# Squares of a fused attention kernel from GpSimd to ScalarE, and the gain vectors' load and product moved

## The chip, the cores and the metric

The kernel runs on one core of one Trainium2 chip. A core has five engines that run their own instruction streams: TensorE (PE, matmuls; PEld is its weight load), VectorE (DVE), ScalarE (ACT), GpSimd (POOL) and SyncE (SP, which here only issues DMAs). Each engine works through its own stream in order; semaphores make one wait for another. DMAs are issued from the queues of SP, ACT and POOL. The metric is the device time of one execution in microseconds (us).

## The reference

```python
def rmsnorm(x, g):
    rms = np.sqrt(np.mean(x * x, axis=-1, keepdims=True) + 1e-06)
    return x / rms * g
# q, k, v: (8, 12, 448, 64); g_q, g_k: (64,)
q_n, k_n = (rmsnorm(q, g_q), rmsnorm(k, g_k))
scores = 1.0 / np.sqrt(64) * np.matmul(q_n, k_n.transpose(0, 1, 3, 2))
attn = np.exp(scores - np.max(scores, axis=-1, keepdims=True))
attn = attn / (np.sum(attn, axis=-1, keepdims=True) + 1e-09)
x = np.matmul(attn, v)          # then reshaped to (3584, 768)
a, b = x @ w1, x @ w2           # (768, 1024) each
h = a * b @ w3                  # (1024, 1024)
return (h @ w_out).astype(np.float32)   # (1024, 768)
```

## The kernel before

The work is cut into 24 groups (`NQ`): 8 batches times 3 sets of 4 heads. The 448 tokens of a head lie on 112 partitions with 4 tokens each (`J`). For a group i the kernel

- loads q and k in float32 (`load_qk`, on SP's queue; three buffers each) and v in bfloat16 (`load_v`, on POOL's queue, four buffers);
- prepares q and k two heads at a time (`pr` 0 and 1): the squares of q and of k (`prep_sq`, tile sq), their sums over 64 elements (`prep_red`, DVE, tile ssq, L166), one over the root by a logarithm and an exponential (`prep_alpha`, ACT, tiles lnv and alpha), three multiplies on DVE (`prep_scale`: qtmp L188, qks L195 with the gains g_b, qks L201), and a transpose to qkT, by PE for the first 5 groups (`prep_pe_transpose`, L220) and by a DMA on SP's queue for the others;
- multiplies q and k (`qk_exp`, PE, tile sc, L235, two PSUM buffers of two banks each) and takes the exponential on ACT (tile P, L244);
- multiplies with ones and with v (`pv_set`, PE, tile pv, L259), and scales the result on DVE into xT (L275) with r, the reciprocal of the row sum, from ACT.

Once a batch has its three groups, its feed-forward part is cut into small pieces ("fillers"): pa = x w1 (L315, copied to a_sb by ACT, L323), pb = x w2 (L332, multiplied with a_sb into abT by DVE, L339), and po = abT times w34 (L354, copied by DVE, L361, and stored through SP's queue). w34 = w3 w_out is made once near the start: w3 is transposed by PE in blocks (`w3_transpose`, L293) and multiplied with w_out (`w34_unit`, L301). The weights w_out, w3, w1 and w2 are loaded through POOL's queue; a copy to the tile gate (L408), which needs the last heads of group 0's k, stands in front of them on POOL.

The order is written out by hand. The program goes through slots, four to a group. A slot holds two score blocks with their exponentials, one set of pv products of the group before, up to two pieces of w34 or of the feed-forward part, and then those parts of the preparation of later groups that the tables PREP and SHIFT put there; for groups 7 and up the squares of pr 0 stand at the end of the last slot of group n - 3, those of pr 1 at the end of the first slot of group n - 2. As each engine runs in order, this also sets the order on ACT, DVE and POOL. `N_SQ_ACT` is the number of groups whose squares go to ACT; those of all other groups go to POOL (L159).

Of the kernel before, what the change touches and what calls it, by code (L numbers as in the profile page):

```python
# [10 lines left out]
MULT = mybir.AluOpType.mult  # L11
# [7 lines left out]
def kernel(  # L19
# [13 lines left out]
    nc = tc.nc  # L33

    B, H, S, D = q.shape
    NP = 112
# [22 lines left out]
    big_pool = ctx.enter_context(tc.tile_pool(name="big", bufs=2))  # L59

    N_PE_T = 5
    N_SQ_ACT = 5
    W34_EV = "DA"
    LAG = 4
    SHIFT = [0, 0, 0, -1, -2, -3, -4]
# [16 lines left out]
    gq_b = const.tile([NP, D], FP, name="gq_b")  # L82
    gk_b = const.tile([NP, D], FP, name="gk_b")
    g_b = const.tile([NP, D], BF, name="g_b")
# [13 lines left out]
    def load_qk(i, split=1, k_eng=None):  # L98
        b, m = divmod(i, NQB)
        s = st[i]  # L100
        s["q"] = load_pool.tile([NP, HQ, J, D], FP, tag="q", name="q_sb")
        s["k"] = load_pool.tile([NP, HQ, J, D], FP, tag="k", name="k_sb")
        n = HQ // split
        for h0 in range(0, HQ, n):
            for t_sb, src, eng in (
                (s["q"], q, nc.sync),
                (s["k"], k, k_eng or nc.sync),
            ):
                eng.dma_start(
                    out=t_sb[:, h0 : h0 + n].rearrange("p h j d -> p h (j d)"),  # L110
                    in_=src[b, HQ * m + h0 : HQ * m + h0 + n].rearrange(
                        "h (p j) d -> p h (j d)", j=J
                    ),
                )
# [24 lines left out]
    def load_wout(nh, c):  # L139
        nc.gpsimd.dma_start(  # L140
            out=w_outs[:, 4 * c : 4 * c + 4, nh * NH : (nh + 1) * NH],
            in_=moe_w_out.rearrange("(c p) n -> p c n", p=128)[
                :, 4 * c : 4 * c + 4, nh * NH : (nh + 1) * NH
            ],
        )
# [24 lines left out]
    def prep_alpha(i, h0=0, h1=HQ):  # L170
        s = st[i]
        if h0 == 0:
            s["lnv"] = prep_pool.tile([NP, 2, HQ, J], FP, tag="lnv", name="lnv")
            s["alpha"] = prep_pool.tile([NP, 2, HQ, J], FP, tag="alpha", name="alpha")
        lnv = s["lnv"][:, :, h0:h1]
        nc.scalar.activation(out=lnv, in_=s["ssq"][:, :, h0:h1], func=AF.Ln, bias=eps_t)
        nc.scalar.activation(  # L177
            out=s["alpha"][:, :, h0:h1], in_=lnv, func=AF.Exp, scale=-0.5
        )

    def prep_scale(i, pr, pe=False):
        s = st[i]
        hs = slice(2 * pr, 2 * pr + 2)
        if pr == 0:
            s["qkT"] = qkT_pool.tile([128, 2, 2 * J, NP], BF, tag="qkT", name="qkT")
        alpha = s["alpha"]
        qtmp = prep_pool.tile([NP, J, 2, D], BF, tag="qtmp", name="qtmp")
        nc.vector.tensor_tensor(  # L188
            out=qtmp.transpose([0, 2, 1, 3]),
            in0=s["q"][:, hs],  # L190
            in1=alpha[:, 0, hs].unsqueeze(3).broadcast_to([NP, 2, J, D]),
            op=MULT,
        )
        qks = prep_pool.tile([NP, 2, J, 2, D], BF, tag="qks", name="qks")
        nc.vector.tensor_tensor(  # L195
            out=qks[:, 0],
            in0=qtmp,
            in1=g_b.unsqueeze(1).unsqueeze(1).broadcast_to([NP, J, 2, D]),
            op=MULT,
        )  # L200
        nc.vector.tensor_tensor(  # L201
            out=qks[:, 1].transpose([0, 2, 1, 3]),
            in0=s["k"][:, hs],
            in1=alpha[:, 1, hs].unsqueeze(3).broadcast_to([NP, 2, J, D]),
            op=MULT,
        )
        if pe:
            s["qks", pr] = qks
        else:
            nc.sync.dma_start_transpose(  # L210
                out=s["qkT"][:, pr], in_=qks.rearrange("p t j h d -> p (t j h d)")
            )
# [183 lines left out]

    with tc.manual_schedule():

        nc.vector.memset(warm_t, 0.0)
        nc.vector.memset(eps_t, 64e-6)  # L400
        nc.vector.memset(ones, 1.0)
        load_qk(0, split=2, k_eng=nc.scalar)
        nc.scalar.dma_start(out=gq_b, in_=g_q.unsqueeze(0).broadcast_to([NP, D]))
        nc.scalar.dma_start(out=gk_b, in_=g_k.unsqueeze(0).broadcast_to([NP, D]))
        nc.scalar.preload_act_table_set("natural_log_exp_and_others")
        load_qk(1)
        make_identity(nc, ident)
        nc.gpsimd.tensor_copy(out=gate, in_=st[0]["k"][:, HQ - 1, 0, 0:1])  # L408
        load_wout(0, 0)
        load_wout(0, 1)  # L410
        for c in range(4):
            load_w3(c)
        load_v(0)
        load_wout(1, 0)
        load_wout(1, 1)
        warm(16)
        nc.vector.tensor_tensor(out=gq_b, in0=gq_b, in1=gk_b, op=MULT)
        nc.vector.tensor_scalar(
            out=g_b, in0=gq_b, scalar1=8.0, scalar2=None, op0=MULT
        )  # L420
        for pr in range(2):
            prep_sq(0, pr, on_act=True)
            prep_red(0, pr)
            prep_alpha(0, 2 * pr, 2 * pr + 2)
            prep_scale(0, pr, pe=True)
            if pr == 0:
                prep_pe_transpose(0, 0)

        wq = [lambda c=c: load_w3(c) for c in range(4, CF)]
        wq.insert(2, lambda: load_v(1))  # L430
        wq.append(lambda: load_v(2))
        for h in range(HQ):
            for half in range(2):
                for w, src in ((w1s, moe_w1), (w2s, moe_w2)):
                    wq.append(
                        lambda w=w, src=src, h=h, half=half: load_w12(w, src, h, half)
                    )
        wq.append(lambda: load_v(3))

        w34q = [lambda: w3_transpose(0), lambda: w3_transpose(1)]  # L440
        for fc in range(CF + LAG):
            if fc < CF:
                w34q.append(lambda fc=fc: w34_unit(fc, 0))
            if fc + 2 < CF:
                w34q.append(lambda fc=fc: w3_transpose(fc + 2))
            if fc >= LAG:
                w34q.append(lambda fc=fc: w34_unit(fc - LAG, 1))

        def prep_part(n, part):
            pe = n < N_PE_T  # L450
            if part[:2] == "sq":
                prep_sq(n, int(part[2]), on_act=n < N_SQ_ACT)
            elif part[:3] == "red":
                prep_red(n, int(part[3]))
            elif part == "alpha":
                prep_alpha(n)
            elif part[:2] == "sc":
                prep_scale(n, int(part[2]), pe=pe)
            elif pe:
                prep_pe_transpose(n, int(part[1]))  # L460


        agenda = {}
        for n in range(1, NQ):
            shift = SHIFT[min(n, len(SHIFT)) - 1]
            table = PREP_1 if n == 1 else PREP
            for part, rel in table.items():
                agenda.setdefault(max(0, 4 * n + rel + shift), []).append((n, part))

        for i in range(NQ + 1):  # L470
            for sl in range(4):
                t = 4 * i + sl
                mine = agenda.pop(t, [])
                for n, part in mine:
                    if part == "load":
                        load_qk(n)
                if i < NQ:
                    qk_exp(i, sl)
                if t == 0:
                    prep_pe_transpose(0, 1)  # L480
                seen = len(fillers)
                if i > 0 and sl < 3:
                    pv_set(i - 1, sl)
                fresh = fillers[seen:]
                if sl == 0 and 4 <= i + 1 < NQ:
                    load_v(i + 1)
                for _ in range(4):
                    if wq:
                        wq.pop(0)()
                if t in W34_SLOTS:  # L490
                    for _ in range(W34_SLOTS[t]):
                        if w34q:
                            w34q.pop(0)()
                elif not w34q:
                    left = (14 - t) % 12 + 1
                    old = len(fillers) - sum(1 for f in fillers if f in fresh)
                    fill(min(2, -(-old // left)))
                for n, part in mine:
                    if part[0] == "t":
                        prep_part(n, part)  # L500
                for n, part in mine:
                    if part[0] != "t" and part != "load":
                        prep_part(n, part)
        fill(len(fillers))
# [28 lines left out]
```

## Time and profile before

| | us |
|---|---|
| median of 3 runs | 411.85 (410.21 to 412.54) |
| profiled execution | 408.66 |
| its span, first to last instruction | 406.6 |
| PE busy | 381.0 (94%) |
| DVE busy | 286.8 (71%) |
| ACT busy | 249.8 (61%) |
| POOL busy | 116.7 (29%) |

The mean granted TensorE clock is 0.977 of full speed. A row of the timeline gives start, duration, engine, line, operation, output and inputs, shapes, count, and in brackets how long the engine stood idle before and what released it. A row of the groups gives busy time and mean time of one in ns, then idle time of the engine ahead of it. A row of the waits gives who waited for whom: total us, times, the longest. A row of the chain of waits gives start, duration and what was waited for. A row of the DMA issues gives the median us from issue to landing.

### The profile page before, as it was taken

The page shows a single profiled execution, that of the slowest core. Times are in us where ns is not written, and L with a number is a line of the kernel's source. Part 1 is how long each engine was busy: PE and PEld are TensorE (multiplying, and loading weights), DVE is VectorE, ACT ScalarE, POOL GpSimd, SP SyncE. Part 2 cuts the span into 40 slices and gives each one's busy share as a digit, 9 for nine tenths or more (in the row PEclk, how much of TensorE's full clock was granted, in tenths as well). Part 3 has the DMA queues.
Part 4 walks back from the last instruction along what each step waited for, and adds up shares of the span by engine and source line. Part 5 has one row for each costly group of instructions (what it writes and reads, how often), then busy time and mean ns, then how long its engine had stood idle before and what let it go on. Part 6 is the DMA issues. An engine that isn't in the chain of part 4 may idle for free.

```text
span 406.6 us, 7530 instructions
## 1 busy us (share of the span) xinstructions
PE 381.0 (94%) x3040; PEld 176.7 (43%) x3040; DVE 286.8 (71%) x383; ACT 249.8 (61%) x391; POOL 116.7 (29%) x135
## 2 busy tenths in 40 slices
PE   5299999999999999998998999998999899999994
PEld 2154554444444444444443443344444444445552
DVE  0686767988789878878987978878887873234232
ACT  2488988776677666675766547665767457751210
POOL 4222443342425504531440341540442300000000
PEclk9579999999999999999999999999999999999999
DMA  7999998357995699647966478457756742003004
GB/s 201 215 233 237 215 205 146 89 93 138 219 174 87 116 179 188 129 114 139 181 130 143 70 209 164 79 117 154 181 109 149 129 115 50 0 2 116 2 20 136
DMA packets 78530, 54.61 MB, mean 134 GB/s; under 512 B 38048, under 2 KB 72352, under 8 KB 78496
## 3 DMA queue, kind: packets, MB, share of 16 engines
q1 hardware_dynamic: 61568, 41.30, 44.3%
q0 software_dynamic: 16192, 12.32, 21.0%
q10 hardware_dynamic: 736, 0.52, 0.5%
q8 instruction: 24, 0.39, 0.4%
q14 instruction: 10, 0.08, 0.1%
HBM read 46.72 MB, written 11.01 MB: 142 GB/s over the span
## 4 chain that ended last, share of the span: by engine, by line
PE 76%; DVE 8%; DMA 8%; issue 4%; ACT 1%; POOL 0%; ACTq 0%; DVEq 0%
PE po L354 17%; PE pa L315 17%; PE pb L332 16%; PE pv L259 13%; PE sc L235 9%; DMA w3s<-in_moe_w_dram 4%; PE wps L301 3%; DMA w_outs<-in_moe_w_out_dram 3%; DVE qks L201 2%; DVE qtmp L188 2%; DVE qks L195 2%; DMA k_sb<-in_k_dram 1%; DVE xT L275 1%; DVE abT L339 1%; PE w3T_ps L293 1%
## 5 line engine op out<-in xcount | busy, mean ns | idle before, releaser
L244 ACT ACTIVATE P<-sc 112x896 bf16<-112x896 f32 x192 | 165.3, 913 | 82.2 <-PE sc L235 82.2
L159 POOL TENSOR_TENSOR sq<-q_sb 112x512 f32<-112x512 f32 x38 | 41.0, 1080 | 159.0 <-DMA q_sb<-in_q_dram 131.1
L332 PE MATMUL pb<-xT,w2s 128*128 128x448 bf16 x384 | 83.1, 352 | 2.1 <-DVE xT L275 2.1
L315 PE MATMUL pa<-xT,w1s 128*128 128x448 bf16 x384 | 83.9, 354 | 0.9 <-DVE xT L275 0.9
L354 PE MATMUL po<-w34s,abT 128*128 128x384 bf16 x448 | 78.5, 327 | 4.3 <-DVE abT L339 4.3
L339 DVE TENSOR_TENSOR abT<-pb,a_sb 128x448 bf16<-128x448 f32 x64 | 39.7, 620 | 55.6 <-PE pb L332 55.2
L166 DVE TENSOR_REDUCE ssq<-sq 112x16 f32<-112x1024 f32 x48 | 58.1, 1210 | 4.8 <-ACT sq L157 4.8
L354 PEld LDWEIGHTS <-abT 128*128 128x128 bf16 x448 | 41.2, 98 | 40.9 <-issue 10.2
L235 PE MATMUL sc<-qkT 64*112 64x448 bf16 x384 | 57.7, 378 | 1.2 <-DVE qkT L223 0.7
L323 ACT CAST a_sb<-pa 128x448 bf16<-128x448 f32 x64 | 33.8, 529 | 36.2 <-PE pa L315 36.2
L332 PEld LDWEIGHTS <-w2s 128*128 128x128 bf16 x384 | 37.6, 98 | 38.5 <-issue 3.7
L315 PEld LDWEIGHTS <-w1s 128*128 128x128 bf16 x384 | 33.0, 98 | 45.1 <-issue 20.3
L201 DVE TENSOR_TENSOR qks<-k_sb,alpha 112x512 bf16<-112x512 f32 x48 | 50.7, 1056 | 0.0
L188 DVE TENSOR_TENSOR qtmp<-q_sb,alpha 112x512 bf16<-112x512 f32 x48 | 45.7, 951 | 6.7 <-ACT alpha L177 6.7
L361 DVE COPY o_sb<-po 128x384 f32<-128x384 f32 x56 | 30.6, 555 | 28.0 <-PE po L354 27.9
L259 PE MATMUL pv<-P,v_sb 112*32 112x448 bf16 x768 | 45.2, 355 | 0.0
L159 POOL TENSOR_TENSOR sq<-k_sb 112x512 f32<-112x512 f32 x38 | 42.8, 1127 | 4.9 <-DMA k_sb<-in_k_dram 4.7
L195 DVE TENSOR_TENSOR qks<-qtmp,g_b 112x512 bf16<-112x512 bf16 x48 | 37.7, 785 | 1.7
L275 DVE TENSOR_TENSOR xT<-pv,r 128x448 bf16<-128x448 f32 x48 | 29.5, 615 | 3.5 <-PE pv L259 3.5
L235 PEld LDWEIGHTS <-qkT 64*112 64x112 bf16 x384 | 17.5, 126 | 32.6 <-issue 29.5
L259 PEld LDWEIGHTS <-v_sb 112*32 112x32 bf16 x768 | 16.1, 96 | 24.1 <-issue 15.5
L301 PE MATMUL wps<-w_outs,w3T 128*128 128x384 bf16 x128 | 23.5, 333 | 0.0
(36 smaller groups left out, 182.8 us busy)
## 6 DMA issues: line engine op xcount, KB each, us to landing
q_sb<-in_q_dram SPq DMA_DIRECT2D x23, 448.0 KB, 5.6
k_sb<-in_k_dram SPq DMA_DIRECT2D x23, 448.0 KB, 6.2
v_sb<-in_v_dram POOLq DMA_DIRECT2D x24, 224.0 KB, 4.8
out_dram<-o_sb SPq DMA_DIRECT2D x8, 336.0 KB, 3.8
out_dram<-o_sb SPq DMA_DIRECT2D x8, 288.0 KB, 3.5
w3s<-in_moe_w_dram POOLq DMA_DIRECT2D x8, 256.0 KB, 15.5
out_dram<-o_sb SPq DMA_DIRECT2D x8, 240.0 KB, 4.1
w_outs<-in_moe_w_out_dram POOLq DMA_DIRECT2D x4, 384.0 KB, 14.0
```

What stands on the lines that cost most here:

```text
L159: nc.gpsimd.tensor_tensor(out=sq[:, t], in0=src[:, hs], in1=src[:, hs], op=MULT)
L166: nc.vector.tensor_reduce(out=s["ssq"][:, :, hs, :], in_=s.pop(("sq", pr)), axis=AX, op=ADD)
L188: nc.vector.tensor_tensor(out=qtmp.transpose([0, 2, 1, 3]), in0=s["q"][:, hs], in1=alpha[:, 0, hs].unsqueeze(3).broadcast_to([NP, 2, J, D] ...
L195: nc.vector.tensor_tensor(out=qks[:, 0], in0=qtmp, in1=g_b.unsqueeze(1).unsqueeze(1).broadcast_to([NP, J, 2, D]), op=MULT,)
L201: nc.vector.tensor_tensor(out=qks[:, 1].transpose([0, 2, 1, 3]), in0=s["k"][:, hs], in1=alpha[:, 1, hs].unsqueeze(3).broadcast_to([NP, 2, ...
L235: nc.tensor.matmul(out=sc[:, u, 0:S], lhsT=qkT[u * D : (u + 1) * D, pr, J + jk, :], rhs=qkT[u * D : (u + 1) * D, pr, 0:J, :].rearrange("d ...
L244: nc.scalar.activation(out=P[:, 2 * pr : 2 * pr + 2, jk, :], in_=sc[:, :, 0:S], func=AF.Exp)
L259: nc.tensor.matmul(out=ps[h * HALF : (h + 1) * HALF, :], lhsT=w, rhs=P[:, h, jk, :], start=(jk == 0), stop=(jk == J - 1), tile_position=(0 ...
L315: nc.tensor.matmul(out=ps[:, 0:S], lhsT=w1s[:, c, fi * 128 : (fi + 1) * 128], rhs=xT[b][:, c, :], start=(c == 0), stop=(c == CM - 1),)
L332: nc.tensor.matmul(out=ps[:, 0:S], lhsT=w2s[:, c, fi * 128 : (fi + 1) * 128], rhs=xT[b][:, c, :], start=(c == 0), stop=(c == CM - 1),)
L339: nc.vector.tensor_tensor(out=abT[bp][:, fi, odd * S : (odd + 1) * S], in0=ps[:, 0:S], in1=a_tiles.pop((b, fi)), op=MULT,)
L354: nc.tensor.matmul(out=ps[:, 0:NH], lhsT=abT[bp][:, fi, t * 128 : (t + 1) * 128], rhs=w34s[:, fi, nh * NH : (nh + 1) * NH], start=(fi == 0 ...
```

## The change

It sets `N_SQ_ACT` to 24, so the squares of all groups run on ACT. The loads of g_q and g_k go from ACT's queue to the front of POOL's (software) queue. Their product, with the factor 8 that makes g_b, moves on DVE from before the first preparation to behind the first sum and alpha of group 0.

```diff
-    N_SQ_ACT = 5
+    N_SQ_ACT = 24
...
+        nc.gpsimd.dma_start(out=gq_b, in_=g_q.unsqueeze(0).broadcast_to([NP, D]))
+        nc.gpsimd.dma_start(out=gk_b, in_=g_k.unsqueeze(0).broadcast_to([NP, D]))
         nc.vector.memset(warm_t, 0.0)
...
         load_qk(0, split=2, k_eng=nc.scalar)
-        nc.scalar.dma_start(out=gq_b, in_=g_q.unsqueeze(0).broadcast_to([NP, D]))
-        nc.scalar.dma_start(out=gk_b, in_=g_k.unsqueeze(0).broadcast_to([NP, D]))
         nc.scalar.preload_act_table_set("natural_log_exp_and_others")
...
         warm(16)
-        nc.vector.tensor_tensor(out=gq_b, in0=gq_b, in1=gk_b, op=MULT)
-        nc.vector.tensor_scalar(
-            out=g_b, in0=gq_b, scalar1=8.0, scalar2=None, op0=MULT
-        )
         for pr in range(2):
             prep_sq(0, pr, on_act=True)
             prep_red(0, pr)
             prep_alpha(0, 2 * pr, 2 * pr + 2)
+            if pr == 0:
+                nc.vector.tensor_tensor(out=gq_b, in0=gq_b, in1=gk_b, op=MULT)
+                nc.vector.tensor_scalar(
+                    out=g_b, in0=gq_b, scalar1=8.0, scalar2=None, op0=MULT
+                )
             prep_scale(0, pr, pe=True)
```

In the steady part of the program, around the turn from one group to the next while pa and pb pieces fill the slots, ACT's row before is this (P are the exponentials, lns and r the reciprocal of the row sum, a_sb the copy of pa):

```order
L244 ACTIVATE P<-sc 112x2x448 x2
L323 CAST a_sb<-pa 128x448
L244 ACTIVATE P<-sc 112x2x448 x2
L269 ACTIVATE lns<-pv 128x448
L271 ACTIVATE r<-lns 128x448
L323 CAST a_sb<-pa 128x448
L244 ACTIVATE P<-sc 112x2x448 x2
L323 CAST a_sb<-pa 128x448
```

And in the changed kernel the same stretch of ACT's row:

```order
L244 ACTIVATE P<-sc 112x2x448 x2
L323 CAST a_sb<-pa 128x448
L157 ACTIVATE sq<-q_sb 112x512
L157 ACTIVATE sq<-k_sb 112x512
L244 ACTIVATE P<-sc 112x2x448 x2
L269 ACTIVATE lns<-pv 128x448
L271 ACTIVATE r<-lns 128x448
L323 CAST a_sb<-pa 128x448
L157 ACTIVATE sq<-q_sb 112x512
L157 ACTIVATE sq<-k_sb 112x512
L244 ACTIVATE P<-sc 112x2x448 x2
L323 CAST a_sb<-pa 128x448
```

A pair of squares now stands in front of the exponentials of the first and of the second slot of a group. On POOL's row only the loads of v are left from there on.

At the start of the program the row of DVE changes so, word for word (before with -, changed with +; ssq are the first sums, g_b the product of the gains):

```order
-L417 TENSOR_TENSOR gq_b<-gq_b,gk_b 112x64
-L418 TENSOR_SCALAR g_b<-gq_b 112x64
-L166 TENSOR_REDUCE ssq<-sq 112x2x8
+L166 TENSOR_REDUCE ssq<-sq 112x2x8
+L422 TENSOR_TENSOR gq_b<-gq_b,gk_b 112x64
+L423 TENSOR_SCALAR g_b<-gq_b 112x64
 L188 TENSOR_TENSOR qtmp<-q_sb,alpha 112x2x4x64
 L195 TENSOR_TENSOR qks<-qtmp,g_b 112x512
```

The product of the gains moved behind the first sums; the first multiply that reads g_b is still L195.

## The prediction

> **What bounds the kernel now.** I read the page's first block, then the list of waits, then the timeline around the longest waits of TensorE (PE). The first block:
>
> ```profile
> span 406.6 us, 7530 instructions
> PE 381.0 (94%) x3040; PEld 176.7 (43%) x3040; DVE 286.8 (71%) x383; ACT 249.8 (61%) x391; POOL 116.7 (29%) x135
> ```
>
> PE is busy for 381.0 of 406.6 us, so a change pays only where it shortens the 25.6 us in which PE stands. The list of waits says for whom it stands (total, times, longest):
>
> ```profile
> PE qkT_ps L220 <- DVE qks L195: 9.9, 3, 7.6
> ...
> PE po L354 <- DVE abT L339: 4.3, 4, 1.3
> ...
> PE pb L332 <- DVE xT L275: 2.1, 2, 1.5
> ...
> PE pa L315 <- DVE xT L275: 0.9, 1, 0.9
> ...
> PE sc L235 <- ACT P L244: 0.4, 2, 0.3
> ```
>
> Two things are left: the head (9.9 us for the first q/k tiles), and seven waits for VectorE (DVE) in the middle, 4.3 + 2.1 + 0.9 = 7.3 us. ScalarE (ACT), to which the work moves, holds PE for 0.4 us only. The first of the seven in the timeline:
>
> ```profile
> 181.53 0.75 POOL L120 DMA_DIRECT2D v_sb<-in_v_dram  x1
> ...
> 181.78 3.10 DVE L201 TENSOR_TENSOR qks<-k_sb,alpha 112x512 bf16<-112x512 f32 x1
> ...
> 182.29 1.05 POOL L159 TENSOR_TENSOR sq<-q_sb 112x512 f32<-112x512 f32 x1
> ...
> 183.29 1.04 POOL L159 TENSOR_TENSOR sq<-k_sb 112x512 f32<-112x512 f32 x1
> ...
> 184.81 0.61 DVE L275 TENSOR_TENSOR xT<-pv,r 128x448 bf16<-128x448 f32 x1
> ...
> 185.34 0.61 DVE L339 TENSOR_TENSOR abT<-pb,a_sb 128x448 bf16<-128x448 f32 x1
> ...
> 186.01 1.64 PE L354 MATMUL po<-w34s,abT 128*128 128x384 bf16 x9 [1.30 <-DVE abT L339]
> ```
>
> A DVE multiply lies beside two GpSimd (POOL) squares for 3.10 us and ends 0.55 us after the second (183.29 + 1.04 = 184.33). Behind it on DVE stand the evacuations xT and abT, and PE waits 1.30 us for abT. The same multiplies early in the program, where ACT takes the squares and POOL only issues loads, and over the whole run:
>
> ```profile
> 27.92 0.72 POOL L120 DMA_DIRECT2D v_sb<-in_v_dram  x1 [2.13 <-DMA v_sb<-in_v_dram]
> 28.00 0.68 DVE L188 TENSOR_TENSOR qtmp<-q_sb,alpha 112x512 bf16<-112x512 f32 x1
> ...
> 29.06 0.68 DVE L201 TENSOR_TENSOR qks<-k_sb,alpha 112x512 bf16<-112x512 f32 x1
> ```
>
> ```profile
> L201 DVE TENSOR_TENSOR qks<-k_sb,alpha 112x512 bf16<-112x512 f32 x48 | 50.7, 1056 | 0.0
> L188 DVE TENSOR_TENSOR qtmp<-q_sb,alpha 112x512 bf16<-112x512 f32 x48 | 45.7, 951 | 6.7 <-ACT alpha L177 6.7
> ```
>
> Alone, or beside a load that POOL issues (27.92), the multiply takes 0.68 us; on average it takes 1.06 and 0.95. So the squares stretch it, not the issue of loads.
>
> **The change part by part.**
>
> *POOL loses its squares.*
>
> ```profile
> L159 POOL TENSOR_TENSOR sq<-q_sb 112x512 f32<-112x512 f32 x38 | 41.0, 1080 | 159.0 <-DMA q_sb<-in_q_dram 131.1 <-DVE ssq L166 13.9 <-DVE abT L339 8.1
> L159 POOL TENSOR_TENSOR sq<-k_sb 112x512 f32<-112x512 f32 x38 | 42.8, 1127 | 4.9 <-DMA k_sb<-in_k_dram 4.7
> ```
>
> These 83.8 us leave POOL, which is on no path. What counts is DVE: 48 x (1.06 - 0.68) = 18 us of L201 and 48 x (0.95 - 0.68) = 13 us of L188 go. DVE is not the bound, so I count only the seven PE waits. With L201 at 0.68, abT of the place above would start some 2.4 us earlier, against a wait of 1.30. The longest of the seven is 1.5, so all go: -7.3 us. Bounds: 0, if something else stretches DVE, to -7.3. I take the full value, since 28.00 shows the lone price beside a load.
>
> *The same squares on ACT.* Price of a pair, from a group whose squares are already there:
>
> ```profile
> 30.21 0.63 ACT L157 ACTIVATE sq<-q_sb 112x512 f32<-112x512 f32 x1
> ...
> 30.74 0.62 ACT L157 ACTIVATE sq<-k_sb 112x512 f32<-112x512 f32 x1
> ...
> 31.26 0.91 ACT L244 ACTIVATE P<-sc 112x896 bf16<-112x896 f32 x1
> ```
>
> The next exponential starts 31.26 - 30.21 = 1.05 us after the pair began. 38 pairs make 40 us; ACT goes from 249.8 to about 290, 73% of the new span. What matters is whether an exponential comes late for PE. Two adjacent slots of a group, in each of which the squares now stand at the slot's end, in front of the next exponentials:
>
> ```profile
> 128.17 1.72 ACT L244 ACTIVATE P<-sc 112x896 bf16<-112x896 f32 x2 [0.75 <-PE sc L235]
> ...
> 131.49 0.59 PE L235 MATMUL sc<-qkT 64*112 64x448 bf16 x4
> ...
> 131.93 1.72 ACT L244 ACTIVATE P<-sc 112x896 bf16<-112x896 f32 x2 [0.58 <-PE sc L235]
> ...
> 132.21 1.21 DVE L166 TENSOR_REDUCE ssq<-sq 112x16 f32<-112x1024 f32 x1
> ...
> 135.25 0.58 PE L235 MATMUL sc<-qkT 64*112 64x448 bf16 x4
> 135.43 0.62 DVE L339 TENSOR_TENSOR abT<-pb,a_sb 128x448 bf16<-128x448 f32 x1 [1.48 <-PE pb L332]
> ```
>
> The first pair fills the 0.75 us of idle and makes the exponentials 0.30 late; the second meets 0.58 and makes the next 0.30 + 1.05 - 0.58 = 0.77 late. They then end at 131.93 + 1.72 + 0.77 = 134.42; the score matmul that needs their PSUM starts at 135.25, so 0.8 us is left. The lateness would have to pass 1.6 us (135.25 - 133.65) to stop PE. ACT stood idle again before the exponentials that follow, so it does not pile up. I put +0.3 us for the places where idle is shorter; bounds 0 and 19 groups x 0.77 = 14.6.
>
> The Trainium skill, page "ScalarE: Activation LUTs", section "Rules for kernel authors", speaks against this move: multiplications belong on VectorE, and an ACT instruction is to be budgeted at about 0.3 us plus 0.83 ns per element. An estimate by that page is 0.72 us for a square of 512, 1.45 for a pair, a lateness of 0.70 + 0.87 = 1.57: just under the 1.6, so the sum would still be the same, but with nothing left; the row's 1.05 decides.
>
> *A new wait of DVE.* The reduction at L166 follows its squares. POOL ran ahead; ACT finishes the second pair about 132.7 (131.93 - 0.58 + 0.30 + 1.05), so the reduction of 132.21 starts 0.5 us later. Behind it stand one xT and abT, and abT itself stood 1.48 us for PE: hidden. If that cover goes, it is those 0.5 us in 19 groups, inside the 14.6 above.
>
> *The g loads and their product.* The head's rows:
>
> ```profile
> 4.82 0.61 ACT L157 ACTIVATE sq<-k_sb 112x512 f32<-112x512 f32 x1
> ...
> 11.26 0.23 DVE L417 TENSOR_TENSOR gq_b<-gq_b,gk_b 112x64 f32<-112x64 f32 x1 [10.08 <-DMA gk_b<-in_g_k_dram]
> ...
> 14.68 1.16 PE L220 MATMUL qkT_ps<-ident,qks 112*128 112x112 bf16 x8 [7.64 <-DVE qks L195]
> ...
> 35.52 0.62 PE L293 MATMUL w3T_ps<-ident,w3s 128*128 128x128 bf16 x8 [0.71 <-DMA w3s<-in_moe_w_dram]
> ```
>
> ```profile
> 7.39 11.97 DMA w_outs<-in_moe_w_out_dram
> ...
> 19.64 15.83 DMA w3s<-in_moe_w_dram
> ```
>
> ```profile
> q_sb<-in_q_dram SPq DMA_DIRECT2D x23, 448.0 KB, 5.6
> ...
> v_sb<-in_v_dram POOLq DMA_DIRECT2D x24, 224.0 KB, 4.8
> ...
> gk_b<-in_g_k_dram ACTq DMA_DIRECT2D x1, 28.0 KB, 8.9
> ```
>
> The squares end at 5.43, but the first reduction stands behind L417, which waits for gk_b until 11.26. Moved behind the reduction, the chain to PE's first transpose (14.68) may start about 6 us earlier. On the software queue g lands between v_sb's 4.8 us and its own 8.9 us after an issue near 1, so at 6 to 10; the product is wanted near 7.3, and the head moves forward by 3 to 6 us. But none of that reaches the end. The chain of waits goes through the loads: w_outs issued at 7.39, then w3s issued at 19.64 and landed at 35.47, and PE's transposes at 35.52 already wait 0.71 us for it. Those issues are POOL's own, opened by the landing of the first k, and the head does not touch them. An earlier head only makes PE wait longer there: 0 us. Bounds: -6, if the loads move with the head, to +5.6, if a q load, whose buffer is freed earlier, passes in full ahead of that w3s. 0 is nearest, since the chain has no step of the head in it. The two issues leave ACT and cost POOL about 0.7 us each (row 27.92) ahead of the identity; the head's 8 us cover that.
>
> *Sum.* -7.3 + 0.3 + 0 = -7.0 us on the span of 406.6: about 399.6. The profiled execution took 408.66 us, 2.1 around its span, and so would take 401.7. The median of the runs before is 411.85, 3.2 above the profiled one; taken from there, 404.9.
>
> **Rivals.**
>
> *The head's gain counts too.* For it: 7.6 us is PE's longest wait. Against it: the w3s row. Time: 404.9 - 6 = 399.
>
> *The stretch is not the squares'.* At 181.53 a load is issued just as L201 begins; were that, or DVE's own operands, the cause, the seven waits stay: 411.85 + 0.3, about 412, and the change does not do what it says. Against it: 27.92 beside 28.00.
>
> *ACT becomes the bound (slower).* A mechanism with one place: squares in front of the exponentials in the last and first slot of a group. If PE waited for the whole lateness in 19 groups, +14.6 - 7.3 = +7.3, 419. It decides where lateness passes 1.6 us, which needs the pair at about 1.45 us, or q landing late in front of it. The page's budget above is just at that edge; the row of 0.63 is against it.
>
> **How the numbers follow.** About 0.5%, 2 us, is what a measurement here can tell from no change. The forecast (403 to 407) has 0.62; the head's gain 0.12; the stretch that stays 0.13; ACT as the bound 0.08; 0.05 for the rest, mostly a part of the gain. Faster: 0.62 + 0.12 + 0.04 = 0.78; same 0.13; slower 0.09. The range from 399.5 to 411 leaves out most of the slower cases and half of the case without effect.
>
> **What would show it.** L201 and L188 near 0.68 us on average; no wait of PE for abT or xT above 0.2 us; w3T_ps still at 35 to 36 us with a longer wait for w3s; a first transpose at 8 to 11 us; PE's wait for P still under 1 us; 1 us of waiting for squares per group on DVE. I would be wrong if L201 stays above 1 us, if that transpose block comes before 34, or if "PE sc <- ACT P" grows past 3 us.

## The result: 398.34 us, and the profile after

The changed kernel takes 398.34 us (median of 4, 398.27 to 398.77) against 411.03 (median of 4, 409.09 to 412.54): 0.970 of the time before, 95% interval 0.965 to 0.974. The forecast was 404.9 in a range from 399.5 to 411: the direction is right, the gain of 12.7 us is nearly twice the one forecast, and the time lies just past the fast end of the range. The ratios here and below leave out runs more than 1.5% above the fastest of their kernel, while medians and spreads hold all runs. The first block of the profile's page:

```profile
span 396.4 us, 7505 instructions
PE 379.8 (96%) x3040; PEld 176.8 (45%) x3040; DVE 243.0 (61%) x383; ACT 286.3 (72%) x467; POOL 35.4 (9%) x61
```

The span fell by 10.2 us: PE's busy time by 1.2, the time in which it stood by 9.0. The groups of the exponential and of the three multiplies:

```profile
L244 ACT ACTIVATE P<-sc 112x896 bf16<-112x896 f32 x192 | 165.2, 915 | 45.3 <-PE sc L235 45.3
...
L188 DVE TENSOR_TENSOR qtmp<-q_sb,alpha 112x512 bf16<-112x512 f32 x48 | 32.8, 682 | 6.4 <-ACT alpha L177 6.4
L201 DVE TENSOR_TENSOR qks<-k_sb,alpha 112x512 bf16<-112x512 f32 x48 | 32.9, 685 | 0.0
...
L195 DVE TENSOR_TENSOR qks<-qtmp,g_b 112x512 bf16<-112x512 bf16 x48 | 20.4, 425 | 1.7
```

L188 and L201 are at their lone price. The third multiply, L195, which the prediction left out, took 785 ns on average before. The list of waits has no row any more in which PE waits for abT or xT, nor for P. The two largest that are left of PE's, and a wait of DVE that grew (from 4.8 us in 5 pieces):

```profile
DVE ssq L166 <- ACT sq L157: 13.0, 17, 4.6
...
PE qkT_ps L220 <- DVE qks L195: 7.4, 4, 4.8
...
PE w3T_ps L293 <- DMA w3s<-in_moe_w_dram: 2.0, 2, 1.1
```

In the steady part squares now stand in front of the exponentials (timeline; the two slots answer to 128.17 and 131.93 of before):

```profile
126.34 0.58 PE L235 MATMUL sc<-qkT 64*112 64x448 bf16 x4
126.44 0.64 ACT L157 ACTIVATE sq<-k_sb 112x512 f32<-112x512 f32 x1
...
126.96 1.73 ACT L244 ACTIVATE P<-sc 112x896 bf16<-112x896 f32 x2
...
130.59 0.62 ACT L157 ACTIVATE sq<-k_sb 112x512 f32<-112x512 f32 x1
...
131.10 1.71 ACT L244 ACTIVATE P<-sc 112x896 bf16<-112x896 f32 x2
131.24 1.22 DVE L166 TENSOR_REDUCE ssq<-sq 112x16 f32<-112x1024 f32 x1 [0.33 <-ACT sq L157]
...
133.87 0.40 PE L235 MATMUL sc<-qkT 64*112 64x448 bf16 x2
```

The exponentials follow the squares without a gap, and end at 132.81, 1.06 us before the score matmul that needs their PSUM: late, and hidden. The head:

```profile
10.55 0.23 DVE L422 TENSOR_TENSOR gq_b<-gq_b,gk_b 112x64 f32<-112x64 f32 x1 [3.52 <-DMA gk_b<-in_g_k_dram]
...
12.12 1.16 PE L220 MATMUL qkT_ps<-ident,qks 112*128 112x112 bf16 x8 [4.81 <-DVE qks L195]
...
20.03 1.03 PE L293 MATMUL w3T_ps<-ident,w3s 128*128 128x128 bf16 x8 [1.05 <-DMA w3s<-in_moe_w_dram]
...
34.14 0.62 PE L293 MATMUL w3T_ps<-ident,w3s 128*128 128x128 bf16 x8 [0.97 <-DMA w3s<-in_moe_w_dram]
```

The first transpose of q and k, at 14.68 before, is 2.6 us earlier; the prediction had put 3 to 6, with the gains landed between 6 and 10 us, but the product waited for gk_b until 10.55. The transposes of the fifth w3 block, at 35.52 before, are 1.4 us earlier, and they wait for their load as before.

### The profile page after: what moved, and what is told of

The parts are those of the page before. It is cut to its first block, busy times and chain, and to the rows that moved or that the text cites. A ratio compares the mean times of both kernels' runs of the same rounds, so it can differ in the third digit from the quotient of the medians.

```text
span 396.4 us, 7505 instructions
## 1 busy us (share of the span) xinstructions
PE 379.8 (96%) x3040; PEld 176.8 (45%) x3040; DVE 243.0 (61%) x383; ACT 286.3 (72%) x467; POOL 35.4 (9%) x61
## 4 chain that ended last, share of the span: by engine, by line
PE 88%; DMA 8%; ACT 1%; DVE 1%; POOL 0%; issue 0%; ACTq 0%
PE pa L315 20%; PE po L354 19%; PE pb L332 18%; PE pv L259 15%; PE sc L235 11%; DMA w3s<-in_moe_w_dram 4%; PE wps L301 3%; DMA w_outs<-in_moe_w_out_dram 3%; DMA k_sb<-in_k_dram 1%; PE w3T_ps L293 1%; PE qkT_ps L220 0%; ACT P L244 0%; DVE qtmp L188 0%; ACT w34s L286 0%; DVE qks L201 0%; ACT sq L157 0%
## 5 line engine op out<-in xcount | busy, mean ns | idle before, releaser
L166 DVE TENSOR_REDUCE ssq<-sq 112x16 f32<-112x1024 f32 x48 | 58.3, 1215 | 13.0 <-ACT sq L157 13.0
L354 PEld LDWEIGHTS <-abT 128*128 128x128 bf16 x448 | 41.5, 98 | 35.6 <-issue 10.2
L120 POOL DMA_DIRECT2D v_sb<-in_v_dram x24 | 17.0, 707 | 243.8 <-PE pv L259 223.8
L188 DVE TENSOR_TENSOR qtmp<-q_sb,alpha 112x512 bf16<-112x512 f32 x48 | 32.8, 682 | 6.4 <-ACT alpha L177 6.4
L201 DVE TENSOR_TENSOR qks<-k_sb,alpha 112x512 bf16<-112x512 f32 x48 | 32.9, 685 | 0.0
L157 ACT ACTIVATE sq<-q_sb 112x512 f32<-112x512 f32 x48 | 30.4, 634 | 1.6 <-DMA q_sb<-in_q_dram 1.6
L157 ACT ACTIVATE sq<-k_sb 112x512 f32<-112x512 f32 x48 | 30.0, 625 | 0.0
```

The costliest lines, as they stand in the source:

```text
L157: nc.scalar.activation(out=sq[:, t], in_=src[:, hs], func=AF.Square)
L166: nc.vector.tensor_reduce(out=s["ssq"][:, :, hs, :], in_=s.pop(("sq", pr)), axis=AX, op=ADD)
L201: nc.vector.tensor_tensor(out=qks[:, 1].transpose([0, 2, 1, 3]), in0=s["k"][:, hs], in1=alpha[:, 1, hs].unsqueeze(3).broadcast_to([NP, 2, ...
L354: nc.tensor.matmul(out=ps[:, 0:NH], lhsT=abT[bp][:, fi, t * 128 : (t + 1) * 128], rhs=w34s[:, fi, nh * NH : (nh + 1) * NH], start=(fi == 0 ...
```

## The experiments

Ratios are to the kernel before, with 95% intervals; experiments that ran together are named. Runs of the kernel before spread over 10 us (403.5 to 413.7 in 23 runs beside the first four experiments), so differences of 1 or 2 us between variants are read from their own runs and from traces, not from the ratios.

**1. The squares alone** (chip 3, with 2, 3 and 4).

```diff
-    N_SQ_ACT = 5
+    N_SQ_ACT = 24
```

> The squares of all groups on ScalarE, the gain vectors loaded and multiplied as before. Theory (the squares on GpSimd stretch the VectorE multiplies, and differently in every execution): TensorE's seven waits in the middle go (7.3 us) with about 0.17 us of pipeline refill behind each (1.2 us), the first w3 wait stays at 35.5 us; span about 398, time about 400 (ratio 0.973 to the kernel before), and the runs lie within 1 us of each other instead of 3.5. Rival (the head gives most of the surplus over the forecast): 403 to 405, spread as before.

400.02 us (399.43 to 400.37, 6 runs), ratio 0.977 (0.973 to 0.981), span 398.1. The runs lie within 0.94 us. So the squares bring most of the gain, and in these runs the spread goes with them. Its w3 transposes stand in the timeline without any wait in front of them:

```profile
21.16 1.04 PE L293 MATMUL w3T_ps<-ident,w3s 128*128 128x128 bf16 x8
...
35.21 0.62 PE L293 MATMUL w3T_ps<-ident,w3s 128*128 128x128 bf16 x8
```

**2. The head alone.**

```diff
-    N_SQ_ACT = 24
+    N_SQ_ACT = 5
```
(in the changed kernel)

> The gain vectors first on the software queue and their product behind the first sum, squares on GpSimd as before. Theory: only what the weight loads allow comes through, 1.4 us at the w3 wait (34.1 instead of 35.5), time about 409.5 (ratio 0.997), spread of some 3 us as before. Rival (the whole 2.6 us by which the first transpose is earlier): 408.4; second rival (the head gives what the forecast lacked): 405 to 406.

409.08 us (404.46 to 410.6, 12 runs), ratio 1.002 (0.997 to 1.006): no difference that can be told beside GpSimd's squares, whose spread covers an effect of 1 us. PE's waits for abT and xT are there again (list of waits):

```profile
PE po L354 <- DVE abT L339: 4.5, 4, 1.1
PE pb L332 <- DVE xT L275: 3.2, 3, 1.4
```

**3. Squares for nobody on GpSimd.** ScalarE delivers all squares; GpSimd computes those of groups 5 to 23 again.

```diff
                 nc.scalar.activation(out=sq[:, t], in_=src[:, hs], func=AF.Square)
+                if i >= 5:
+                    idle = prep_pool.tile([NP, 2, J, D], FP, tag="idle", name="idle")
+                    nc.gpsimd.tensor_tensor(
+                        out=idle, in0=src[:, hs], in1=src[:, hs], op=MULT
+                    )
```

> The changed kernel, and GpSimd squares q and k of groups 5 to 23 once more into a tile that nobody reads, so ScalarE still delivers the sums' input. Theory (GpSimd reading SBUF holds up the multiplies): L201 and L188 go back to 0.9 to 1.1 us on average, TensorE waits for abT and xT again, 403 to 409 us and a wider spread. Rival (what cost time was that VectorE's sums waited for GpSimd's squares, or the place of the squares in the chain): 398.3, multiplies may stretch without any loss.

410.16 us (406.64 to 416.54, 12 runs), ratio 1.000 (0.996 to 1.004). The whole gain is gone, though nothing waits for these squares but a later load into the same q and k buffers; the list of waits has no wait of PE for a q or k load. Groups by line (L193 and L206 are L188 and L201 of the other kernels), and a row of the waits:

```profile
L193 DVE TENSOR_TENSOR qtmp<-q_sb,alpha 112x512 bf16<-112x512 f32 x48 | 50.6, 1054 | 7.0 <-ACT alpha L182 7.0
L206 DVE TENSOR_TENSOR qks<-k_sb,alpha 112x512 bf16<-112x512 f32 x48 | 50.0, 1041 | 0.0
```

```profile
PE po L359 <- DVE abT L344: 5.0, 4, 1.5
```

The means mix two kinds of places. Laid side by side in the trace, L201's instruction (L206 here) takes 1.75 us on average in the 16 places where it overlaps one of these squares and 0.68 in the other 32; in the kernel before it is 1.87 in 15 places and 0.68 in the rest. The xT multiply, which has one input in PSUM, takes 0.61 to 0.62 us and the reduction 1.21, beside a square or not.

**4. No gains at all** (their loads left out, both set to one, so the result lacks them).

```diff
-        nc.gpsimd.dma_start(out=gq_b, in_=g_q.unsqueeze(0).broadcast_to([NP, D]))
-        nc.gpsimd.dma_start(out=gk_b, in_=g_k.unsqueeze(0).broadcast_to([NP, D]))
+        nc.vector.memset(gq_b, 1.0)
+        nc.vector.memset(gk_b, 1.0)
```

> The changed kernel without the loads of g_q and g_k: both are set to one by VectorE (the gains are left out of the result). Theory (the head is hidden behind the w3 load): first transpose near 8.6 us instead of 12.1, but the wait for w3 at 34 us stays and grows; 398.3 within 0.5. Rival (the head counts): 398.3 - 3.5 = 394.8.

397.04 us (396.56 to 398.23, 6 runs), ratio 0.969 (0.965 to 0.974); span 396.5, as the changed kernel's 396.4. The timeline:

```profile
8.87 0.37 PE L220 MATMUL qkT_ps<-ident,qks 112*128 112x112 bf16 x4 [1.62 <-DVE qks L195]
...
20.38 0.93 PE L293 MATMUL w3T_ps<-ident,w3s 128*128 128x128 bf16 x7 [4.84 <-DMA w3s<-in_moe_w_dram]
```

The first transpose is 3.3 us earlier than in the changed kernel, and PE waits for w3 instead. But the wait that grows is that of the first block at 20 us, not the one at 34 that I had expected, which is gone here. The median is 1.3 us under that of the changed kernel, which ran in another session. The profiled execution was the slowest of the six (398.23; the others 396.56 to 397.17), so its span does not stand for them. The median lies between theory (398.3) and rival (394.8), and this experiment does not settle the head.

**5. GpSimd busy without reading** (chip 3 again, a later session, with 6, 7 and 8).

```diff
+                    idle = prep_pool.tile([NP, 2, J, D], FP, tag="idle", name="idle")
+                    nc.gpsimd.memset(idle, 0.0)
```
(in the place of experiment 3's squares)

> The changed kernel, and GpSimd fills a tile that nobody reads four times per group (groups 5 to 23), so GpSimd is busy but reads no SBUF. Theory (the multiplies are held up only by a GpSimd instruction that reads SBUF): L201 and L188 stay at 0.68 us, 398.3 within 1. Rival (any busy GpSimd holds VectorE): L201 above 0.75 us, waits for abT and xT back, 400 to 404.

398.95 us (398.27 to 399.97, 4 runs), ratio 0.971 (0.966 to 0.977). Groups by line (L204 is L201), then two rows of the timeline (L191 is L188):

```profile
L160 POOL MEMSET idle<- 112x512 f32 x76 | 36.8, 543 | 0.0
...
L204 DVE TENSOR_TENSOR qks<-k_sb,alpha 112x512 bf16<-112x512 f32 x48 | 32.9, 685 | 0.0
```

```profile
109.21 1.94 POOL L160 MEMSET idle<- 112x512 f32 x4
...
110.12 0.68 DVE L191 TENSOR_TENSOR qtmp<-q_sb,alpha 112x512 bf16<-112x512 f32 x1
```

76 fills of the same tile size do not stretch the multiplies. The fills are half as long as the squares (0.54 against 1.1 us), but they do meet them: the multiply at 110.12 lies wholly beside fills and takes 0.68 us, and of 11 multiplies that overlap a fill none takes longer than its lone price. With 3 as the counterpart, it is the squares' reading and not GpSimd's being busy that stretches them, unless a square differs from a fill in something else that counts. The Trainium skill, page "SBUF — State Buffer", section "Who interferes with whom", says that a VectorE instruction with two SBUF inputs contends with a GpSimd instruction that reads SBUF, not with one that only writes, and that tensor_reduce never does; the traces agree: 1041 against 685 ns for L201, and 1213 against 1215 ns for the reduction in 3 and 5.

**6. Every square twice on ScalarE.**

```diff
+                    nc.scalar.activation(out=idle, in_=src[:, hs], func=AF.Square)
```
(in the same place)

> The changed kernel with each square of groups 5 to 23 taken a second time on ScalarE into a tile that nobody reads: four in a slot, 2.1 us. Theory (1.6 us of lateness is what the scores' PSUM forgives): lateness 1.35 and then 1.35 + 2.1 - 0.58 = 2.9 us, so TensorE stands about 1.3 us in each of some 13 groups, 17 us in all: about 412 to 416, and 'PE sc <- ACT P' shows it. Rival (ScalarE has room for more, since it stood idle 45 us for scores in the changed kernel): 399 to 402.

413.88 us (412.41 to 415.83, 10 runs), ratio 1.008 (1.005 to 1.011), against 398.95 for experiment 5 on the same chip. The wait that I had named as the slower rival appears, and PE's busy time, in which refills and a slower clock count, grows by 6.2 us:

```profile
PE sc L238 <- ACT P L247: 7.9, 24, 0.7
```

```profile
PE 386.0 (94%) x3040; PEld 180.5 (44%) x3040; DVE 244.2 (59%) x383; ACT 321.4 (78%) x543; POOL 35.3 (9%) x61
```

The time came out as expected, its parts did not: 7.9 us of waits in 24 pieces where I had put 17. The middle of the program (the table further down) is 13.8 us longer than in the changed kernel: the waits, and 5.6 us of PE's busy time behind them. Four squares in a slot are past the lateness that is forgiven; two are not.

**7. w3 first among the weight loads.**

```diff
-        load_wout(0, 0)
-        load_wout(0, 1)
-        for c in range(4):
-            load_w3(c)
-        load_v(0)
-        load_wout(1, 0)
-        load_wout(1, 1)
+        load_w3(0)
+        load_w3(1)
+        load_wout(0, 0)
+        load_wout(0, 1)
+        load_w3(2)
+        load_w3(3)
+        load_w3(4)
+        load_v(0)
...
-        wq = [lambda c=c: load_w3(c) for c in range(4, CF)]
-        wq.insert(2, lambda: load_v(1))
+        wq = [lambda c=c: load_w3(c) for c in range(5, CF)]
+        wq.append(lambda: load_wout(1, 0))
+        wq.append(lambda: load_wout(1, 1))
+        wq.append(lambda: load_v(1))
```

> The changed kernel with another order of the weight loads on the software queue: w3 blocks 0 and 1 ahead of the first halves of w_out, then w3 2 to 7 and v, and the second halves of w_out last. Theory (the head's gain stops at the landing of w3): TensorE's waits of 1.05 us at 20.0 and 0.97 at 34.1 go, 396.3 (span 394.4). Rival (the sum of bytes is the wall, so the wait moves to another load): 398.3.

397.36 us (396.8 to 398.2, 6 runs), ratio 0.967 (0.963 to 0.971), span 395.3 against 396.4; the runs lie below those of 5 on the same chip. Half of the expected gain. Both waits for w3 are gone; the first block starts right behind the second score product, so PE's own chain from the first transpose is the next limit:

```profile
18.71 1.04 PE L293 MATMUL w3T_ps<-ident,w3s 128*128 128x128 bf16 x8
```

**8. The gain vectors in front of q and k.** Experiment 7, with

```diff
-        nc.gpsimd.dma_start(out=gq_b, in_=g_q.unsqueeze(0).broadcast_to([NP, D]))
-        nc.gpsimd.dma_start(out=gk_b, in_=g_k.unsqueeze(0).broadcast_to([NP, D]))
+        nc.sync.dma_start(out=gq_b, in_=g_q.unsqueeze(0).broadcast_to([NP, D]))
+        nc.scalar.dma_start(out=gk_b, in_=g_k.unsqueeze(0).broadcast_to([NP, D]))
```

> The same order of weight loads, and g_q and g_k first on the queues of SyncE and ScalarE, ahead of q and k. Theory (with w3 out of the way the head counts): first transpose at 9 to 9.5 us instead of 12.1, and 1 to 2.5 us less than with the new order alone: 394 to 395.5. Rival (another wall behind it): the same as with the new order alone.

402.32 us (401.84 to 402.88, 6 runs), ratio 0.979 (0.975 to 0.983): 5 us slower than 7. Timeline, the third row from further on:

```profile
8.37 0.63 ACT L157 ACTIVATE sq<-q_sb 112x512 f32<-112x512 f32 x1 [4.89 <-DMA q_sb<-in_q_dram]
...
10.50 0.18 POOL L408 COPY gate<-k_sb 112x1 f32<-112x1 f32 x1 [9.19 <-DMA k_sb<-in_k_dram]
...
26.95 1.44 PE L301 MATMUL wps<-w_outs,w3T 128*128 128x384 bf16 x4 [2.19 <-DMA w_outs<-in_moe_w_out_dram]
```

Two loads of 28 KB in front delay q and k: the first square starts at 8.37 instead of 4.62, and the gate, which opens the weight loads, at 10.50 instead of 6.44. PE then waits 2.19 us for w_out, and its granted clock, 0.50 until 24 us in 7, is 0.50 until 32 here. My expectation was wrong.

**9. The changed kernel again** (chip 1, with 10 and 11).

> The changed kernel as it is, on the same chip as the next two, so that they can be set against it: 398.3, within 0.5.

399.19 us (398.24 to 401.7, 6 runs), ratio 0.973 (0.969 to 0.978), span 397.8. The runs spread over 3.5 us, where the first four had 0.5. The first w3 block came at 21.0 us, and the fifth when its load let it:

```profile
35.48 0.62 PE L293 MATMUL w3T_ps<-ident,w3s 128*128 128x128 bf16 x8 [1.14 <-DMA w3s<-in_moe_w_dram]
```

In the first execution of the same kernel it was 34.14, in the kernel before 35.52. So the changed kernel is itself uncertain by about 1 us, and the 1.4 us that it had won at this block are not there the second time.

**10. Gains on ScalarE's queue, the product moved.**

```diff
-        nc.gpsimd.dma_start(out=gq_b, in_=g_q.unsqueeze(0).broadcast_to([NP, D]))
-        nc.gpsimd.dma_start(out=gk_b, in_=g_k.unsqueeze(0).broadcast_to([NP, D]))
...
         load_qk(0, split=2, k_eng=nc.scalar)
+        nc.scalar.dma_start(out=gq_b, in_=g_q.unsqueeze(0).broadcast_to([NP, D]))
+        nc.scalar.dma_start(out=gk_b, in_=g_k.unsqueeze(0).broadcast_to([NP, D]))
```

> The changed kernel with the loads of g_q and g_k back on ScalarE's queue behind k; the squares on ScalarE and the product behind the first sum stay. Theory (of the head it is the moved product that counts, the queue moves the landing of g_k by 0.7 us only and w3 hides that): first transpose near 12.8 us, first w3 block still near 20, 398.3 to 398.8. Rival (the queue makes it): 400, as with the squares alone.

399.48 us (399.05 to 400.78, 6 runs), ratio 0.973 (0.969 to 0.977): the same as 9. The first transpose came at 12.95 us: the queue moved that transpose by 0.8 us and the place of the product by the rest of the 2.6. Neither reaches the fifth w3 block, which waits 1.02 us for its load and starts at 34.92. What the queue does change is the end: from the start of the last 64 po matmuls to the end of the span the traces have 15.6 to 15.7 us where gains come through the queues of ScalarE or SyncE (before, 1, 8 and 10), and 15.3 in all others. Why, no trace shows.

**11. A version that beats both.** Experiment 7, with one row of each gain loaded on one partition and spread by a matmul with ones.

```diff
-        nc.gpsimd.dma_start(out=gq_b, in_=g_q.unsqueeze(0).broadcast_to([NP, D]))
-        nc.gpsimd.dma_start(out=gk_b, in_=g_k.unsqueeze(0).broadcast_to([NP, D]))
+        nc.gpsimd.dma_start(out=g_row[:, 0], in_=g_q.unsqueeze(0))
+        nc.gpsimd.dma_start(out=g_row[:, 1], in_=g_k.unsqueeze(0))
...
+                g_ps = mm_psum.tile([NP, D], FP, tag="mm", name="g_ps")
+                nc.tensor.matmul(
+                    out=g_ps, lhsT=one_row, rhs=g8_row, start=True, stop=True
+                )
+                nc.vector.tensor_copy(out=g_b, in_=g_ps)
```

> The changed kernel with the w3 blocks first on the software queue, and the gains loaded as one row each on one partition; their product is spread over the partitions by a matmul with ones. Theory (112 short packets for each gain vector make it land late): the rows land before 6 us, the first transpose comes at 9 to 9.5 us instead of 12, the first w3 block at its landing near 16; 395 to 396 against 397.4 with the order of loads alone. Rival (loads of w3 hide it): 397.4.

396.04 us (395.7 to 398.27, 6 runs), ratio 0.965 (0.961 to 0.969): 3.2 us below the changed kernel on the same chip, in the medians. Timeline (L222 and L295 are L220 and L293), then the loads:

```profile
10.16 1.16 PE L222 MATMUL qkT_ps<-ident,qks 112*128 112x112 bf16 x8 [1.38 <-DVE qks L197]
...
16.95 1.04 PE L295 MATMUL w3T_ps<-ident,w3s 128*128 128x128 bf16 x8
```

```profile
g_row<-in_g_q_dram POOLq DMA_DIRECT2D x1, 0.2 KB, 5.5
g_row<-in_g_k_dram POOLq DMA_DIRECT2D x1, 0.2 KB, 5.8
```

The rows landed later than expected (5.8 us after issue, against 8.5 for the broadcast of g_k in the changed kernel), and the first transpose is at 10.2 instead of 9.5.

## Why the prediction was right or wrong

PE's matmuls come in the same order in all kernels, so a span can be cut at the same two matmuls: the first transpose of the eighth w3 block, and the first of the 64 po matmuls that close the program.

| profiled execution (us) | start | middle | end | span |
|---|---|---|---|---|
| kernel before | 46.6 | 344.4 | 15.7 | 406.6 |
| changed kernel | 45.2 | 335.9 | 15.3 | 396.4 |
| squares alone (1) | 46.5 | 335.9 | 15.6 | 398.1 |
| head alone (2) | 45.6 | 345.0 | 15.3 | 405.9 |
| squares for nobody (3) | 47.5 | 344.9 | 15.3 | 407.7 |
| ScalarE twice (6) | 46.8 | 349.7 | 15.3 | 411.8 |
| changed kernel again (9) | 46.6 | 335.9 | 15.3 | 397.8 |

**Right: the mechanism in the middle.** GpSimd's squares stretched the multiplies; without them the seven waits are gone, and the middle is 335.93 us, to 0.01, in the changed kernel and in experiments 1, 4, 5 and 7 to 11. Experiment 3 shows it in the other direction. The rival in which the issue of loads holds VectorE is refuted by the changed kernel itself: 24 loads of v are still issued there, and L201 takes 685 ns beside them as elsewhere.

**Wrong by 3.2 us, the largest part: "taken from there".** I carried the 3.2 us between the profiled execution (408.66) and the median of 411.85 over to the changed kernel as if it belonged to the measurement. The changed kernel's median lies 0.04 us above its profiled execution (398.34 and 398.30). Measured on the gain, the medians of the four runs of each kernel moved by 12.7 us, the profiled executions by 10.4. The runs tie the difference to the squares: with them on GpSimd, groups of 11 to 23 runs spread over 6 to 11 us (5 to 6 among the runs that the ratios count), without them groups of 4 to 10 runs over 0.5 to 3.5. The granted clock does not explain it: the kernel before took 403.49 us at 0.977 and 413.22 at 0.979. That the longer executions lose their time in waits of the same kind is likely but not shown; there is no trace of one.

**Wrong by 1.1 us: the price of a wait.** The step "so all go: -7.3 us" counted the gaps alone, but the middle lost 8.4. A wait in the middle of a block costs PE more than the gap. In the trace of before, 16 matmuls of po without a wait:

```profile
240.98 2.77 PE L354 MATMUL po<-w34s,abT 128*128 128x384 bf16 x16
```

and the interrupted block, whose second part (9 matmuls, 1.64 us at 186.01) stands in the prediction:

```profile
183.40 1.31 PE L354 MATMUL po<-w34s,abT 128*128 128x384 bf16 x7
```

1.31 + 1.64 = 2.95, so 0.18 us more than the gap, seven times 1.2 to 1.3 us. In the middle alone PE's busy time fell by 1.2 us (336.6 to 335.5). The fall over the whole span (381.0 to 379.8) is no measure of it: experiment 1, whose middle has no such wait either, has 381.2.

**The head, "0 us": the wall was right, its landing was not fixed.** The prediction named the load of the fifth w3 block, landed at 35.47, as what an earlier head would run into. PE does wait for it in all seven traces that have the moved product and the old order of weight loads, by 0.8 to 2.5 us, and starts the block between 34.1 and 36.5 us. What failed is the fixed landing. POOL issues this load when a part of w_out has landed, at 19.64 before and at 19.01 and 19.83 in the two executions of the changed kernel, and it landed 1.4 us earlier than before in the first and at the same time in the second. So the 1.4 us of the start are a part of the measured gain, but not shown to be the head's:

| kernel | first w3 block | fifth | PE's wait before the fifth |
|---|---|---|---|
| before | 21.5 | 35.5 | 0.7 |
| squares alone (1) | 21.2 | 35.2 | none |
| changed kernel | 20.0 | 34.1 | 1.0 |
| changed kernel again (9) | 21.0 | 35.5 | 1.1 |
| gains on ScalarE's queue (10) | 20.8 | 34.9 | 1.0 |
| w3 first (7) | 18.7 | 32.8 | none |
| w3 first, gain rows (11) | 17.0 | 31.3 | none |

Once w3 is loaded first the wall is gone and an earlier head counts. By medians the head is worth 0.8 us (9 against 1, on different chips) to 1.7 (the result against 1), 0.4 of it from the end of the program, which the prediction did not have. The rival "the head's gain counts too" named 399 and lies nearest to the result, but by luck: the squares alone give 400.02, the head alone 409.08.

**Nearly right: ScalarE.** +0.3 us for late exponentials; the changed kernel's trace has no such wait, so 0. The lateness computed was 0.77 us; in the trace the exponentials start at 131.10, 1.00 us behind their score product (130.10), where before it was 0.44 (131.49 to 131.93): 0.56 us late, with 1.06 to spare. Experiment 6 lies beyond the edge. The estimate from the budget of the Trainium skill, page "ScalarE: Activation LUTs", section "Rules for kernel authors" (1.45 us for a pair), would have put the changed kernel at that edge; 1.05 was the better figure, and the pair that starts at 130.05 in the changed kernel takes 1.05 again.

Sum on the span: 8.4 in the middle, 1.4 at the start and 0.4 at the end are the measured 10.2. On the time, 404.9 was 6.6 us too high: 3.2 carried over, 1.1 for the price of the waits, 1.4 at the start, 0.4 at the end, 0.3 for late exponentials, and 0.2 because the changed kernel's profiled execution lies 1.9 us above its span and not 2.1.

## What to carry to other kernels

A profiled execution that is quicker than the median is a hint: if a mechanism is suspected of varying from run to run, its price in the median can be larger than in the trace, and removing it can remove that difference too. Count a wait of PE as its gap and what the interrupted block loses besides. Cut two traces at the same instructions before crediting a gain to a cause, and profile the same kernel twice before crediting a load that landed earlier. Moving elementwise work from GpSimd to a less loaded engine paid here through a third engine, VectorE, so look there for what it is worth.

## What was not expected of the hardware

Broadcasting a vector of 64 floats to 112 partitions by DMA is dear for its 28 KB. The second vector took 8.5 us to landing on the software queue, where one row of it took 5.8 (experiment 11), and 8.9 on ScalarE's queue behind k. In front of q and k the two held these up by 3.7 to 4.1 us (experiment 8; 4.62 to 8.37 and 6.44 to 10.50).

The start runs at half clock. In every trace the granted clock is 0.50 from 14 to 20 us, and it is back at 1.00 by 28 us in all but experiment 8; the eight transposes of a w3 block take 1.03 us in the kernel before at 21.46 and 0.62 at 35.52.
